# One task graph for everything behind the second run, and fold weights converted straight into SBUF

## The chip, the cores and the metric

The kernel runs on one core of a Trainium2 chip. The metric is the device time of one execution in microseconds. The kernel before takes 986.05 us, the median of three runs (982.78 to 986.43). The profile shown here is of one execution of 987.92 us; its span, from the first to the last instruction, is 986.2 us, so 1.7 us lie outside.

## What is computed

Three stages follow one another: a recurrent attention with a decaying state (4 batches, 8 heads, 768 steps, head size 48), and two gated blocks over the 3072 rows of 384 features that it gives.

```
state = zeros(B, H, D, D)
for t in range(S):                          # S = 768
    cur = einsum('bhd,bhe->bhde', u * k[t], v[t])
    y[t] = einsum('bhd,bhde->bhe', r[t], state + cur)
    state = w * state + einsum('bhd,bhe->bhde', k[t], v[t])
x = y as (3072, 384)
m = ((x @ w_a) * (x @ w_b)) @ w_out         # 384 -> 1536 -> 384
h = ((m @ w1) * (m @ w2)) @ w3              # 384 -> 1024 -> 1024
return h @ w_out2                           # 1024 -> 384
```

The MoE weights arrive as 64-bit floats. The kernel turns them into 32-bit ones with integer operations and then splits every matmul operand into a high part in fp32r and a low part (the rest), so that a product takes three matmuls: high by high, high by low, low by high.

## The kernel before

The sequence is cut into six chunks of 128 steps. A **unit** is one batch of one chunk (24 units; chunk 0 is done apart, so 20 go through the general path). A unit's attention is a chain: the scores on TensorE (L485), mask and diagonal on VectorE (L496, L502), the product with the state and with v on TensorE (L521, L525), evacuation as high and low part into `xt` (ScalarE L561 and L562, VectorE L563 and L564), the state update (TensorE L586, ScalarE L593, VectorE L603). GpSimd prepares r, k and the diagonal for the next unit (L457 to L478). When four units are done, six small DMAs (L570, `y_shuffle`) bring the odd rows of `xt` in place.

The **first block** works chunk by chunk (q = 0 to 5). For each of 12 feature tiles f, `ab_mm` makes two banks of 9 matmuls each (L736), ScalarE and VectorE multiply and split them (L755, L761, L762, L767), and `m_mm` adds 9 matmuls into the three banks `m` (L789 to L791). A finished chunk goes to DRAM (`m_d`).

The **second block** doesn't use w1 and w2 as they are: sums of slices of them (`T_OPS`, five groups g, `sums`) are multiplied with sums of slices of m (`S_OPS`), which saves matmuls; and w3 and the last weights are multiplied with each other once, in eight **folds** of 24 matmuls (L1079), so that one product (L1262 to L1264, called o here) remains. It runs over three pairs of chunks (L1159).

Weights are converted by `Stream`: SyncE loads a `raw` tile of 512 KB, VectorE makes the 32-bit value in three operations (L112, L126, L129), ScalarE rounds the high part and makes two checks (L142, L148, L163), VectorE makes the low part (L162). In the second half of the stream (`add_second`) there are 34 such conversions: 12 of w1 and w2, 6 of the last weights (`wo2`) and 16 of w3 (`w3T`). All results go to DRAM: w1 and w2 to `w12_d`, from where `sums` loads them again, the others with their two parts to `wo2_d` and `w3_d`, from where they come back for the folds.

What sets the order: up to chunk q = 4 of the first block everything is written out by hand. A list of runs (0 with its first six tiles; 1; 0 with the other six; 2; 3; 4) gives the main sequence, `merge` puts the slots of the next chunk's attention between its slots in equal steps, and the steps of conversions and sums likewise (`late`). From q = 5 on, everything (the last chunk, the folds, the second block) is a list of `Task`s with engine, duration, dependencies, buffers and a priority. The function `plan` orders them greedily: again and again it gives an engine the ready task that can start first, ties by priority. A task's end may be later than the engine's time for it by `extra`, which stands for a DMA's flight. Between the two parts the pools `att` and `stg` are released, and a pool `mid` takes their place.

Each engine runs its own instructions strictly in the order in which they were written.

## Time and profile before

| | us |
|---|---|
| median of three runs | 986.05 |
| profiled execution | 987.92 |
| its span | 986.2 |
| TensorE busy / VectorE busy / ScalarE busy / GpSimd busy | 895.8 / 569.4 / 370.7 / 240.7 |
| mean granted clock of TensorE | 0.947 |

The engines' busy times are sums over the span and hide that it has stretches with different limits. In the table of stretches each engine has its busy time and in brackets its number of instructions; PEclk is the granted clock of TensorE, where 1.00 is its upper level of 2.4 GHz. A matmul record is longer than the time that a matmul takes in a row of them, since matmuls are pipelined; what one takes is read from the chain, where a row of n of them stands with its whole duration.

### The profile page before, as it was taken

What the parts mean: (1) busy time and instruction counts of PE and PEld (TensorE: products, weight loads), DVE (VectorE), ACT (ScalarE), POOL (GpSimd) and SP (SyncE); (2) the same over time, 40 slices, a digit from 0 to 9 for tenths busy, and PEclk for the clock granted to TensorE, in tenths of its full rate; (3) what the DMA queues carried; (4) which work ended last, traced back from release to release, by engine and by line L of the source; (5) the groups of instructions that cost most, each with busy time, mean ns of one, the idle gap of its engine ahead of it and who ended that gap; (6) DMA issues with size and microseconds to landing.
All of it is one profiled execution on the core that took longest, in us unless ns stands there. A gap on an engine that the chain in (4) does not pass through costs nothing.

```text
span 986.2 us, 13053 instructions
## 1 busy us (share of the span) xinstructions
PE 895.8 (91%) x4827; PEld 747.3 (76%) x4827; DVE 569.4 (58%) x901; ACT 370.7 (38%) x830; POOL 240.7 (24%) x242
## 2 busy tenths in 40 slices
PE   8777999978796888999999967999999999999996
PEld 7566788867664666888888856888878788888996
DVE  8998964467676884545444403223569757845442
ACT  3554654235344544333232212223335233333232
POOL 2213200044020220645144001111534523212010
PEclk9888999989878788999999988999999999999998
DMA  8454531167578677325442381422655634324001
GB/s 264 162 174 137 154 107 43 47 212 190 174 249 241 210 218 204 141 82 182 128 142 81 104 308 68 158 96 96 230 156 164 197 116 131 107 91 155 6 33 67
DMA packets 55846, 143.60 MB, mean 146 GB/s; under 512 B 5536, under 2 KB 22688, under 8 KB 55776
## 3 DMA queue, kind: packets, MB, share of 16 engines
q1 hardware_dynamic: 55776, 142.70, 45.3%
q8 instruction: 40, 0.66, 0.3%
q14 instruction: 30, 0.25, 0.1%
HBM read 106.11 MB, written 34.60 MB: 143 GB/s over the span
## 4 chain that ended last, share of the span: by engine, by line
PE 60%; DVE 14%; DMA 14%; ACT 5%; issue 4%; POOL 1%; SPq 1%; DVEq 0%; ACTq 0%; POOLq 0%
PE ab L736 21%; PE ab L1159 9%; PE m L789 3%; PE m L791 3%; PE m L790 3%; PE at L1159 3%; PE at L1079 3%; DMA raw<-in_w3T_dram 3%; PE o L1262 3%; PE o L1263 3%; PE o L1264 3%; DVE cvt L126 2%; DMA raw<-in_wo_dram 2%; DMA r<-m_d 2%; DMA raw<-in_w_dram 1%
## 5 line engine op out<-in xcount | busy, mean ns | idle before, releaser
L762 ACT CAST gh<-ab 128x512 fp32r<-128x512 f32 x60 | 35.2, 587 | 167.9 <-DVE ab L761 151.8
L789 PE MATMUL m<-gh,woh 128*128 128x512 f32 x216 | 87.9, 407 | 2.5 <-DVE g L797 2.0
L1232 DVE TENSOR_TENSOR qx<-qx,ab 128x512 f32<-128x512 f32 x101 | 67.6, 685 | 39.1 <-PE ab L1159 31.8
L791 PE MATMUL m<-gh,wol 128*128 128x512 f32 x216 | 86.0, 398 | 0.8 <-DVE wol L162 0.8
L790 PE MATMUL m<-gl,woh 128*128 128x512 f32 x216 | 86.4, 400 | 0.0
L761 DVE TENSOR_TENSOR ab<-g,ab 128x512 f32<-128x512 f32 x60 | 41.7, 696 | 73.4 <-PE ab L736 72.5
L457 POOL TENSOR_TENSOR rk<-rk,tr 112x512 f32<-112x512 f32 x16 | 22.0, 1377 | 251.6 <-DMA rk<-in_rkT_dram 156.0
L1170 POOL TENSOR_TENSOR qx<-qx,qx 128x512 f32<-128x512 f32 x30 | 41.9, 1405 | 145.6 <-DVE qx L1232 135.2
L1254 DVE TENSOR_TENSOR gl<-qx,gh 128x512 fp32r<-128x512 f32 x48 | 37.5, 782 | 46.3 <-ACT gh L1252 46.2
L736 PE MATMUL ab<-xt,wab0h 128*128 128x512 f32 x144 | 50.5, 434 | 13.0 <-DVE gl L767 10.7
L755 ACT COPY g<-ab 128x512 f32<-128x512 f32 x60 | 34.9, 582 | 71.7 <-PE ab L736 71.7
L1252 ACT CAST gh<-qx 128x512 fp32r<-128x512 f32 x48 | 29.8, 621 | 80.1 <-PE o L1263 78.3
L736 PE MATMUL ab<-xt,wab1h 128*128 128x512 f32 x144 | 49.7, 429 | 9.5 <-ACT g L1034 9.5
L1226 ACT ACTIVATE qx<-ab 128x512 f32<-128x512 f32 x60 | 35.6, 599 | 57.1 <-PE ab L1159 26.7
L767 DVE TENSOR_TENSOR gl<-ab,gh 128x512 fp32r<-128x512 f32 x60 | 41.3, 689 | 26.7 <-ACT gh L762 26.6
L112 DVE TENSOR_SCALAR cvt<-raw 128x512 int32<-128x512 int32 x61 | 29.4, 481 | 45.5 <-DMA raw<-in_w3T_dram 18.2
L789 PEld LDWEIGHTS m<-gh,woh 128*128 128x128 f32 x216 | 41.7, 193 | 13.2 <-DVE g L797 2.5
L791 PEld LDWEIGHTS m<-gh,wol 128*128 128x128 f32 x216 | 41.8, 193 | 10.3 <-DVE wol L162 1.2
L1141 POOL TENSOR_TENSOR qx<-r 128x512 f32<-128x512 f32 x18 | 26.4, 1479 | 92.3 <-DMA m_d<-qx 33.4
L126 DVE SCALAR_TENSOR_TENSOR cvt<-raw,cvt 128x512 int32<-128x512 int32 x61 | 47.8, 784 | 1.2
L790 PEld LDWEIGHTS m<-gl,woh 128*128 128x128 f32 x216 | 41.7, 193 | 8.3
L736 PE MATMUL ab<-xt,wab3h 128*128 128x512 f32 x144 | 46.5, 404 | 0.0
(274 smaller groups left out, 2330.7 us busy)
## 6 DMA issues: line engine op xcount, KB each, us to landing
tg<-t_d SPq DMA_DIRECT2D x45, 640.0 KB, 3.9
natt<-in_nat_dram SPq DMA_DIRECT2D x20, 576.0 KB, 6.1
rk<-in_rkT_dram SPq DMA_DIRECT2D x24, 448.0 KB, 5.1
raw<-in_wab_dram SPq DMA_DIRECT2D x18, 512.0 KB, 3.9
raw<-in_w3T_dram SPq DMA_DIRECT2D x16, 512.0 KB, 4.9
w_d<-s SPq DMA_DIRECT2D x16, 512.0 KB, 3.6
w<-w_d SPq DMA_DIRECT2D x16, 512.0 KB, 4.4
t_d<-s SPq DMA_DIRECT2D x15, 512.0 KB, 2.6
```

The lines of the kernel that those rows point to most:

```text
L126: nc.vector.scalar_tensor_tensor(out=f, in0=w[:, :, 1], scalar=-0x40000000, in1=f, op0=ALU.bitwise_and, op1=ALU.bitwise_or)
L736: mm(ps, lhsT=w[i][:, k, cs], rhs=x[:, j, k, :], start=(n == 0), stop=(n == 3 * KD - 1))
L761: nc.vector.tensor_tensor(out=t["b"], in0=g, in1=t["b"], op=ALU.mult)
L767: nc.vector.tensor_tensor(out=gl, in0=t["b"], in1=gh, op=ALU.subtract)
L789: mm(m_ps[q][k], lhsT=wh[:, j, cs], rhs=gh, start=first, stop=False)
L790: mm(m_ps[q][k], lhsT=wh[:, j, cs], rhs=gl, start=False, stop=False)
L791: mm(m_ps[q][k], lhsT=wl[:, j, cs], rhs=gh, start=False, stop=last)
L1159: mm(bank, lhsT=x, rhs=y, start=(start and n == 0), stop=(stop and n == 2), skip_group_check=True)
L1170: mu = use(task(eng, D_TT if inner else D_P, lambda e=e, dst=dst, xa=xa, xb=xb: e.tensor_tensor(out=dst(), in0=xa(), in1=xb(), op=ALU.mult ...
L1226: e = use(task("ACT", D_A, lambda bv=bv, b=bank[c], s=s: nc.scalar.activation(out=bv.ap, in_=b.ap, func=ACTF.Copy, scale=float(s)), [pt], ...
L1232: e = use(task("DVE", D_TT, lambda bv=bv, b=bank[c], s=s: nc.vector.tensor_tensor(out=bv.ap, in0=bv.ap, in1=b.ap, op=ALU.add if s > 0 else ...
L1254: lo = use(task("DVE", D_TT, lambda x=x, bh=bh: nc.vector.tensor_tensor(out=bh.ap[1], in0=x(), in1=bh.ap[0], op=ALU.subtract), [hi], p0), ...
```

## The change

From the third run on (0 with its other six tiles) everything goes into the same list of tasks: the attention units of chunks 2 to 5 (priority -1000 and upwards, ahead of everything), the chunks 0, 2, 3, 4 and 5 of the first block (`block1`), the 12 conversions of w1 and w2 and the sums made of them (priority 9000, behind everything), and then what was planned already. The first two runs stay as they were.

- `plan` knows a DMA's size: transfers queue behind one another at 5 us per MB and land 2 us later; `extra` is gone.
- The sums of weight slices go from GpSimd (L827) to VectorE, slice by slice (128x128): 72 additions, and 80 splits into two parts with a store of 128 KB each, where there were 22 splits of up to four slices.
- The last weights and w3 are converted into the SBUF tiles that the folds read. `wo2_d` and `w3_d` are gone, and with them 11.5 MB written and 11.5 MB read. Their conversions have priorities around those of chunk q = 5.
- `att` is released by a task (`freed`) that waits for all units and all sums; `stg` stays. The second block's inputs are in other, smaller tiles.
- The o products have priorities inside the second block's groups instead of behind all of them; the last of the eight is cut by batches, so that the first batch can be evacuated earlier.
- The count of the checks becomes a task of the second block.

```diff
-        t.end = at + t.dur + t.extra
+        t.end = at + t.dur
+        if t.size:
+            dma = max(dma, t.end) + t.size * DMA_MB
+            t.end = dma + DMA_0
...
-        runs = [(0, range(SPLIT), 1), (1, range(NF1), None), (0, range(SPLIT, NF1), 2)]
-        runs += [(q, range(NF1), q + 1) for q in range(2, NB - 1)]
+        runs = [(0, range(SPLIT), 1), (1, range(NF1), None)]
...
+        for u in range(U0, NU):
+            c, b = divmod(u, B)
+            pu = -1000.0 + 10 * u
...
+            sc = use(task("PE", 1.35, lambda u=u, bt=bt: picked(bt, lambda: scores(u)), ready_r.get(u, []) + after, pu, bt),
+                     rk_b[u])
...
+                ev = use(task("DVE", 0.84, lambda u=u, h=h: a_diag(u, h), [ev] + ready_d.get(u, []), pu), ba, dg_b[u])
+            by = Buf(at_s, none)
+            y = use(task("PE", 2.3, lambda u=u, by=by: picked([by], lambda: y_mm(u)), [ev] + s_up.get(u - B, []), pu + 1,
+                         [by]), rk_b[u], nat_b[u], ba)
...
+                x_in[c].append(use(task("SP", 0.4, lambda c=c: y_shuffle(c), list(x_in[c]), pu + 3, size=0.13),
+                                   x_b[c], y3_b[c]))
...
+        for n, (q, fs) in enumerate([(0, range(SPLIT, NF1))] + [(q, range(NF1)) for q in range(2, NB)]):
+            mb = Buf(m_s, none)
+            t_ab, t_m = block1(q, fs, 200.0 * n, x_b[q], x_in.get(q, []), mb, [m_last])
...
+            ld = task("SP", 0.1, load, loads[-1:], prio, [br], size=0.52)
+            loads.append(ld)
+            x = use(task("DVE", 0.52, b1, [ld], prio, [bc]), br)
+            x = use(task("DVE", 0.80, b2, [x], prio), br, bc)
+            x = use(task("DVE", 0.80, b3, [x], prio), br, bc)
+            s = use(task("ACT", 0.85, square, [ld], prio, [bq]), br)
+            s = use(task("ACT", 0.90, sign, [s], prio), bq)
...
+            h = use(task("ACT", D_A, hi, [x] + list(after), prio, into if not after else []), bc, *into)
+            return use(task("DVE", 0.8, lo, [h], prio), bc, *into)
...
-            ops = list(ops_on(get, nc.gpsimd, L_OPS if left else T_OPS))
...
+                t = use(task("DVE", 0.25, add, [x[1], y[1]], prio, [b] if new else []), x[2], y[2], b)
...
+        freed = task("none", 0.0, hand_over, units + sum_tasks, 0)
...
+            wo2_l.append(convert(N_SUM + j, flat(wo2)[:, j * 512:(j + 1) * 512], None, R5 - 60 + 2 * j,
+                                 lambda i=i, z=z: [t[:, z * 512:(z + 1) * 512] for t in wo2_get(i)], after=[freed]))
...
+                ld.append(convert(N_SUM + 6 + 2 * i + j, flat(w3T[i])[:, s], None, R5 - 40 + 12 * i + j,
+                                  lambda b3=b3, s=s: [flat(t)[:, s] for t in b3.ap], [b3], after=ld))
...
-                    ot = use(task("PE", 12 * 0.177, go, [lo, fold_end[f]] + ([ot] if z else []), base + 5000 + 10 * n + z,
-                                  [bo] if z == 0 else []), bh, bo)
+                    p0, deps = base + (240 + 40 * z if n == 0 else 950 + 36 * z), [lo, fold_end[f]]
```

How the instructions move is read at three places. The first is VectorE in chunk q = 2 of the first block, while chunk 3's attention runs. Before, conversions of w3 stand there with their low parts (L162), each triple closed up between the product and the split of one feature tile (L761, L767):

```order
L162 TENSOR_TENSOR s<-cvt,s 128x512
L112 TENSOR_SCALAR cvt<-raw 128x512
L126 SCALAR_TENSOR_TENSOR cvt<-raw,cvt 128x512
L129 SCALAR_TENSOR_TENSOR cvt<-raw,cvt 128x512
L761 TENSOR_TENSOR ab<-g,ab 128x512
L162 TENSOR_TENSOR s<-cvt,s 128x512
L112 TENSOR_SCALAR cvt<-raw 128x512
L126 SCALAR_TENSOR_TENSOR cvt<-raw,cvt 128x512
L129 SCALAR_TENSOR_TENSOR cvt<-raw,cvt 128x512
L767 TENSOR_TENSOR gl<-ab,gh 128x512
```

In the changed kernel it is conversions of w1 and w2 (L1062, L1066, L1070), one operation at a time where the unit's chain (L504, L510, L582, L583, L622) leaves room:

```order
L914 TENSOR_TENSOR ab_2411<-g_2429,ab_2411 128x512
L1066 SCALAR_TENSOR_TENSOR cvt<-raw,cvt 128x512
L504 TENSOR_TENSOR a_sc<-at,mask 128x512 x2
L510 COPY_PREDICATED a_sc<-ident,dg 128x512 x2
L919 TENSOR_TENSOR gl_2459<-ab_2411,gh_2458 128x512
L914 TENSOR_TENSOR ab_2465<-g_2475,ab_2465 128x512
L1070 SCALAR_TENSOR_TENSOR cvt<-raw,cvt 128x512
L479 TENSOR_REDUCE dg<-pr 128x8
L919 TENSOR_TENSOR gl_2499<-ab_2465,gh_2498 128x512
L582 TENSOR_TENSOR y_2255<-at,y_2255 112x128
```

What moved: the sixteen w3 conversions left this place, and the attention's operations stand ahead of the rest of a triple.

The second place is ScalarE at the start of chunk q = 5. Before, the first high parts of the second block's inputs (L1150, which read `r`, the loaded m) stand between the chunk's first evacuation of a bank (L1034) and the next steps of its tiles (L1037, L1034):

```order
L1008 COPY qx_4823<-m_4222 128x512
L1034 COPY g_4840<-ab_4813 128x512
L1150 CAST qxa<-r 128x512 x3
L1037 CAST gh_4861<-ab_4829 128x512
L1034 COPY g_4875<-ab_4846 128x512
L1037 CAST gh_4890<-ab_4864 128x512
```

In the changed kernel the chunk's evacuations (L913, L916) and fold weights' high parts (L1083, which read a converted tile) share the place, and the first input of the second block (L1341) comes only behind three folds' evacuations (L1269):

```order
L916 CAST gh_4854<-ab_4797 128x512
L913 COPY g_4857<-ab_4808 128x512
L916 CAST gh_4871<-ab_4844 128x512
L913 COPY g_4883<-ab_4860 128x512
L1083 CAST w_4895<-cvt 128x512
L1269 CAST wf0h<-at_4821 128x384
L1083 CAST w_4895<-cvt 128x512
L913 COPY g_4945<-ab_4920 128x512
L916 CAST gh_4959<-ab_4885 128x512
```

What moved: the instructions that wait for the loaded m left the front of ScalarE's queue, and ones that wait for VectorE's conversions came in.

The third place is SyncE's queue at the same point. Before, it issues all fold weights (L1056, L1070) and the second block's first inputs (L1130) in a row:

```order
L890 DMA l_d<-s 128x256
L1056 DMA wo_4780<-wo_d 128x1536
L1056 DMA wo_4782<-wo_d 128x1536
L1056 DMA wo_4784<-wo_d 128x1536
L1056 DMA wo_4786<-wo_d 128x1536
L1070 DMA w_4788<-w_d_72 128x1024
L1070 DMA w_4789<-w_d_72 128x1024
L1070 DMA w_4792<-w_d_73 128x1024
L1070 DMA w_4793<-w_d_73 128x1024
L1115 DMA tl<-l_d 128x1280
L1130 DMA r<-m_d_58 128x3x256 x2
L1130 DMA r<-m_d_59 128x3x256 x2
```

In the changed kernel the last `y_shuffle` (L589) is followed by five input tiles in pieces (L1319) and by raw weights (L1057):

```order
L589 DMA xt<-y_4055 16x2x512 x6
L1319 DMA qs_4360<-m_d_58 128x256
L1319 DMA qs_4360<-m_d_59 128x256
L1319 DMA qs_4360<-m_d_58 128x256
L1319 DMA qs_4360<-m_d_59 128x256
L1319 DMA qs_4368<-m_d_58 128x256
L1319 DMA qs_4368<-m_d_59 128x256
L1319 DMA qs_4368<-m_d_58 128x256
L1319 DMA qs_4368<-m_d_59 128x256
L1319 DMA qcvt_4384<-m_d_58 128x256
L1319 DMA qcvt_4384<-m_d_59 128x256
L1057 DMA raw<-in_wo_dram 128x512 x2
```

What moved: 1.3 MB of pieces and two raw tiles stand where 7.5 MB of whole tiles stood.

## Rows read from the trace of the kernel before

**Rows 1.** The page: busy time, share of span, instructions.
```profile
PE 895.8 (91%) x4827; PEld 747.3 (76%) x4827; DVE 569.4 (58%) x901; ACT 370.7 (38%) x830; POOL 240.7 (24%) x242
```
**Rows 2.** Table of stretches: start:end, length, busy (instructions), PEclk, DMA, GB/s.
```profile
core 0: us, PE busy (x) PEld busy (x) DVE busy (x) ACT busy (x) POOL busy (x), PEclk, DMA share, GB/s
183.25:398.42 215.17, 175.79 (x978) 139.54 (x978) 146.68 (x240) 96.44 (x251) 49.45 (x45) 0.87 0.65 200
398.42:565.00 166.58, 166.58 (x978) 136.36 (x977) 76.26 (x126) 53.25 (x122) 65.02 (x95) 1.00 0.38 127
565.00:597.04 32.04, 18.12 (x71) 14.08 (x69) 5.69 (x15) 6.38 (x12) 1.15 (x1) 0.80 0.75 279
597.04:705.00 107.96, 107.96 (x508) 94.34 (x509) 32.65 (x48) 26.20 (x48) 21.28 (x15) 0.98 0.34 113
705.00:986.20 281.20, 267.02 (x1279) 231.44 (x1277) 168.73 (x237) 95.99 (x167) 72.81 (x51) 0.99 0.36 116
```
**Rows 3.** The same table for the first block's first matmuls (line 736).
```profile
183.25:398.42 215.17, 93.62 (x343) 69.32 (x343) 0.87 0.65 200
398.42:565.00 166.58, 99.50 (x411) 76.25 (x411) 1.00 0.38 127
```
**Rows 4.** The same table for instructions on the banks m; PE first.
```profile
183.25:398.42 215.17, 45.13 (x171) 33.40 (x171) 1.88 (x3) 1.56 (x3) 0.87 0.65 200
398.42:565.00 166.58, 49.49 (x199) 36.71 (x198) 0.00 (x0) 3.31 (x6) 1.00 0.38 127
```
**Rows 5.** Chain that ended last: start, us, what; rows of equal matmuls.
```profile
177.09 4.12 PE ab L736 x18
...
611.68 4.19 PE at L1079 x24
```
**Rows 6.** Waits from 183.25 to 398.42: who <- whom: us, times, longest.
```profile
POOL rk L457 <- DMA rk<-in_rkT_dram: 112.1, 6, 34.0
...
DVE cvt L112 <- DMA raw<-in_w3T_dram: 18.2, 12, 3.4
ACT s L142 <- DMA w_d<-s: 17.6, 7, 6.0
...
PE at L485 <- DVE s L603: 11.7, 4, 5.2
...
PE ab L736 <- DVE gl L767: 10.7, 2, 5.8
PE at L525 <- DVE a_sc L502: 9.6, 5, 4.5
```
**Rows 7.** Chain that ended last, from 568 to 597 us.
```profile
568.70 2.63 DMA l_d<-s
...
574.16 10.79 DMA w<-w_d
...
584.97 9.83 DMA r<-m_d
...
594.87 1.14 ACT qxa L1150 x2
```
**Rows 8.** Groups of instructions: busy us, mean ns, idle before and its releasers.
```profile
L112 DVE TENSOR_SCALAR cvt<-raw 128x512 int32<-128x512 int32 x61 | 29.4, 481 | 45.5 <-DMA raw<-in_w3T_dram 18.2 <-DMA raw<-in_w_dram 15.5 <-DMA raw<-in_wo_dram 6.7
L126 DVE SCALAR_TENSOR_TENSOR cvt<-raw,cvt 128x512 int32<-128x512 int32 x61 | 47.8, 784 | 1.2
L129 DVE SCALAR_TENSOR_TENSOR cvt<-raw,cvt 128x512 int32<-128x512 int32 x61 | 45.4, 745 | 1.2
L827 POOL TENSOR_TENSOR tw<-wa 128x128 f32<-128x128 f32 x32 | 15.0, 501 | 97.2 <-DMA wa<-w_d 94.3 <-DVE gl L767 2.9
```
**Rows 9.** Single lines: duration ns min/median/max, first and last start.
```profile
L889 DVE TENSOR_TENSOR s<-tw,s x22: 282/692/1402, 408.7 to 569.2; 128x512 fp32r<-128x512 f32 x16, 128x384 fp32r<-128x384 f32 x5, 128x128 fp32r<-128x128 f32 x1
L1152 DVE TENSOR_TENSOR qw4l<-qx,qw4h x5: 685/1181/1793, 668.3 to 834.1; 128x512 fp32r<-128x512 f32 x5
L570 SPq DMA_DIRECT2D xt<-y x30: 585/592/762, 98.2 to 558.1; - x30
```
**Rows 10.** Timeline at the end: start, us, engine, line, operation [idle before].
```profile
977.78 0.34 PE L1264 MATMUL o<-wf1h,gl 128*128 128x384 f32 x1
979.48 0.48 ACT L1277 COPY qx<-o 128x384 f32<-128x384 f32 x1 [2.42 <-DMA out_dram<-qx]
979.99 0.56 DVE L1275 COPY qx<-o 128x384 f32<-128x384 f32 x1 [2.27 <-ACT qx L1277]
```

More of the change, by code (lines that the diff above doesn't have):

```diff
@@ L278, in rwkv_moe_kernel @@
     l_d = dram.tile([128, 5, 2, 128], F32, name="l_d")
-    wo2_d = dram.tile([128, 2, NF2 * DM], F32, name="wo2_d")
-    w3_d = [dram.tile([128, 2, NF2 * 128], F32, name=f"w3_d{i}") for i in range(NF2)]
     def flat(ap):
@@ L898, in rwkv_moe_kernel, with task, use, run_tasks @@
-        second = []
+        tasks = []
+        def task(*a, **k):
+            t = Task(*a, **k)
+            for b in t.bufs:
+                b.users.append(t)
+            tasks.append(t)
+            return t
+        def use(t, *bufs):
+            for b in bufs:
+                b.users.append(t)
+            return t
+        def run_tasks():
+            plan(tasks)
+            for t in tasks:
+                t.end = 0.0
+            tasks.clear()
+        D_TT, D_A, D_P, MM = 0.70, 0.60, 1.45, 0.2275
@@ new lines, in rwkv_moe_kernel, with g_get, gg_get, ps_get @@
+        CONV = 9000.0
+        def g_get(key):
+            return gp.tile([128, TB], F32, tag=key, name=key)
+        def gg_get(key):
+            return tuple(gp.tile([128, TB], F32R, tag=f"g{p}{key}", name=f"g{p}{key}") for p in "hl")
+        def ps_get(key):
+            return psp.tile([128, 512], F32, tag=key, name=key)
+        def none(key):
+            return key
+        banks = [Slot(f"ab{k}") for k in range(3)]
+        at_s = [Slot(f"at{k}") for k in range(2)]
+        g_s = [Slot(f"g{k}") for k in range(2)]
@@ new lines, in rwkv_moe_kernel, with m_close, ev @@
+        gg_s = [Slot(k) for k in range(3)]
+        m_s = [Slot(("m0", "m1", "m2"))]
+        def m_close(q, m, mb, prio, pool, get):
+            out = []
+            for k in range(KD):
+                b = Buf(pool, get)
+                def ev(k=k, b=b):
+                    if q == 0:
+                        nc.vector.tensor_tensor(out=b.ap, in0=m_ps[q][k], in1=m_part[0][:, k, :], op=ALU.add)
+                    else:
+                        nc.scalar.copy(out=b.ap, in_=m_ps[q][k])
+                e = use(task("ACT" if q else "DVE", D_A if q else D_TT, ev, [m], prio, [b]), mb)
+                out.append(use(task("SP", 0.1, lambda k=k, b=b: nc.sync.dma_start(out=m_d[q][:, k, :], in_=b.ap), [e],
+                                    prio, size=0.256), b))
+            return out
@@ L916, in rwkv_moe_kernel @@
                 late += [lambda: None] * (len(late) // LATE)
-            if n == 2:
-                st.split(len(st.jobs))
-                k = len(st.jobs)
-                add_second()
-                second = [step] * (len(st.jobs) - k + 2)
-                for g in range(NG + 1):
-                    second += sums(g)
-            if n >= 2:
-                share = len(second) * len(main) // sum(
-                    3 * len(r[1]) for r in runs[n:]) if n < len(runs) - 1 else len(second)
-                late, second = second[:share], second[share:]
@@ new lines, in rwkv_moe_kernel, with put @@
+        first = len(st.jobs)
+        N_SUM = first + 4 * KD
+        for i in range(4):
+            for k in range(KD):
+                def put(f, i=i, k=k):
+                    for x in range(2):
+                        nc.sync.dma_start(
+                            out=w12_d[4 * i + x:4 * i + x + 3:2, :, k, :].rearrange("j p c -> p j c"),
+                            in_=f[:, x * 256:(x + 1) * 256].rearrange("p (j c) -> p j c", j=2))
+                done[i, k] = convert(first + i * KD + k, w12[i, :, k, :], put, CONV + 100 * i + k)
@@ L1047, in rwkv_moe_kernel @@
-        md_last = m_close(q, m_t[NF1 - 1], 10 * NF1)
-        f_dep = []
-        w_t, wo2_t, w3_t = {}, {}, {}
-        def wo2_load(p, i):
-            def go():
-                t = wo2_t[p, i] = mid.tile([128, 4, DM], F32R, tag=f"x{2 * p + i}", name=f"wo2{p}{i}")
-                nc.sync.dma_start(out=flat(t).bitcast(F32), in_=wo2_d[:, p, i * 4 * DM:(i + 1) * 4 * DM])
-            return task("SP", 0.1, go, [], -5, extra=5)
-        wo2_l = [wo2_load(p, i) for p in range(2) for i in range(2)]
@@ L1061, in rwkv_moe_kernel, with wo2_get @@
-        w3_s = [Slot(k) for k in range(2)]
+        R5 = 200.0 * (NB - 2)
+        ab_b, m_t, md_last = t_ab, t_m, d
+        o_slot = Slot(("m0", "m1", "m2", "at1"))
+        w_t, wo2_t = {}, {}
+        def wo2_get(i):
+            if i not in wo2_t:
+                wo2_t[i] = [mid_p[0].tile([128, 4, DM], F32R, tag=f"x{2 * i + p}", name="wo2") for p in range(2)]
+            return [flat(t) for t in wo2_t[i]]
+        wo2_l = []
+        for j in range(6):
+            i, z = divmod(j, 3)
+            wo2_l.append(convert(N_SUM + j, flat(wo2)[:, j * 512:(j + 1) * 512], None, R5 - 60 + 2 * j,
+                                 lambda i=i, z=z: [t[:, z * 512:(z + 1) * 512] for t in wo2_get(i)], after=[freed]))
```

489 lines of the change are left out of this document (302 added, 187 removed).

## The prediction

> **What bounds the kernel now.** I read the page's busy times first: TensorE is busy for 91% of the span, nothing else for more than 58% [rows 1]. So TensorE's own work is the floor, and the question is where it is not working, or working at its lower clock. The table by stretches answers that [rows 2]. I cut it where the program changes: up to 183.25 us the first two runs, which stay as they are; to 398.42 the stretch of chunks 0 and 2 of the first block in which all 34 late conversions run; to 565 the next chunks with sums; to 597 the change of pools; to 705 chunk 5 with the folds; then the second block. From 398 to 565 and from 597 to 705 TensorE is busy all the time at a clock of 1.00 and 0.98. From 183 to 398 it is busy for 176 of 215 us at 0.87, and from 565 to 597 for 18 of 32 us at 0.80. The second block loses little. The waits then say what the first bad stretch lacks [rows 6]: TensorE stands before scores, products and `ab` for VectorE, and VectorE stands before a conversion for its raw tile (L112) while ScalarE waits for the store of an earlier result. These waits of a few us each sit in queues that the attention's chain shares. In the second bad stretch the chain is one piece [rows 7]: a store of sums (2.6 us), then 10.8 us for the fold weights and 9.8 us for the loaded m, and then ScalarE's first split of that m, behind which the evacuations of chunk 5 are queued.
>
> **What TensorE needs.** A row of 18 matmuls of 512 columns takes 4.12 us, 0.229 us each; a row of 24 of 384 columns takes 4.19 us, 0.175 us each [rows 5]. The price of the attention comes from the stretch without idle time: 166.58 us less 411 + 199 = 610 matmuls [rows 3, 4] at 0.229 us (139.7 us) leaves 26.9 us for the other 978 - 610 = 368, or 0.073 us each [rows 2]. With that each stretch has a floor at the full clock:
>
> - 183 to 398: 343 + 171 = 514 matmuls give 117.7 us, 464 of attention 33.9 us: 151.6 us instead of 215.2, so 63.6 us too long.
> - 398 to 565: 166.6 us, nothing to gain.
> - 565 to 597: 69 of its 71 matmuls are of 512 columns: 15.8 us instead of 32.0, 16.2 us too long.
> - 597 to 705: 508, of which 8 x 24 = 192 are folds: 72.4 + 33.6 = 106.0 us instead of 108.0.
> - From 705: 1279, of which 3 x 2 x 8 x 12 = 576 are o: 161.0 + 100.8 = 261.8 us, then 8.1 us from the last matmul to the end [rows 10]; instead of 281.2, 11.3 us too long.
>
> With 183.25 us ahead, the floor is 183.25 + 151.6 + 166.6 + 15.8 + 106.0 + 261.8 + 8.1 = 893.2 us of span. No TensorE work is taken away; all that the change can do is to come nearer to that.
>
> **The change, part by part.** *One graph instead of merged lists.* In the stretch from 183 to 565 the units' operations come first and everything else fills in. Whether a plan holds on the chip can be read from the part that is planned already: from 597 on, 2.0 + 11.3 = 13.3 us are lost on 367.8 us of work, 3.6%. The task durations written in the code lie near the trace's for what I can compare (a conversion's first operation 0.52 against 0.48 us, the other two 0.80 against 0.78 and 0.75 [rows 8]). I take 3.6% of the 334.0 us from 183 to 597: **12 us** lost where 79.8 were. Bounds: 0 (the stretch from 398 on lost nothing, with the same units and tiles), and all of the 79.8.
>
> *What runs beside the attention.* VectorE was busy for 147 of 215 us there [rows 2]. Of the conversions only the 12 of w1 and w2 and the first of `wo2` remain, at 0.48 + 0.78 + 0.75 = 2.0 us each [rows 8], and no low parts but those of the sums. The 22 of w3 and `wo2` that are moved cost VectorE 2.0 + 0.69 = 2.7 us each [rows 8, 9], some 59 us, which go out of a stretch where VectorE is late and into chunk 5, where it is busy for 33 of 108 us.
>
> *Sums on VectorE.* GpSimd took 0.50 us for one addition [rows 8]. On VectorE no such row exists; a split of one slice took 0.28 us, one of four 0.69 [rows 9]. I take 0.28 for 72 additions and 80 splits: 43 us instead of 15, spread over the 330 us of chunks 0 to 4. That adds 9% to VectorE's load there and is hidden as long as VectorE's queue isn't late; nothing in the 398 to 565 stretch (76 of 167 us busy) speaks against it. ScalarE splits slices too and was busy for a third of its time.
>
> *SyncE.* The 58 further stores and the pieces of m make 379 DMAs in all where there were 339. One issue takes SyncE 0.59 us in `y_shuffle`, whose six take 3.6 us [rows 9]; the plan counts 0.4 us for them and 0.1 for others. So a chunk's `xt` lands some 3 us later than planned. Behind the shuffle on SyncE stand the next units' r, k and v. For chunks 3 to 5 the attention is done early (its priority is ahead of all), which hides it; for chunk 2, whose block follows at once, I count **2 us**, inside the 12.
>
> *The change of pools.* Chunk 5 no longer waits for 7.5 MB: five input pieces and the raw tiles are queued, and ScalarE has the splits of m far behind. The 10.8 + 9.8 us go. Next late there would be the conversions themselves: 18 remain behind `freed`, each a load, three operations, a split, with two raw tiles. In the 215 us from 183 on, 34 were done, 6.3 us each at most; 18 at 6.3 us are 113 us against 106 us of TensorE's work. VectorE's load is 18 x 2.7 + 4 x 0.7 for the first `wo2` tiles + 33 = 84 of 106 us. That is tight but it is spread by priorities over the chunk, so I add **3 us** (bounds 0 and 113 - 106 + one fold's 4.2, so 11).
>
> VectorE's operations on two SBUF tiles beside GpSimd stretch from 0.69 to 1.79 us in L1152 [rows 9]; with 15 GpSimd additions in chunk 5 that is up to 15 x 1.1 = 16 us more for VectorE, the upper bound again. The Trainium skill (SBUF — State Buffer, Who interferes with whom) says that a VectorE instruction with two SBUF inputs and a GpSimd instruction that reads SBUF block each other for the whole instruction; it speaks against moving the sums and conversions to VectorE beside GpSimd's work. By it the sum would have 84 + 16 = 100 of 106 us, still no bound of its own, some 8 instead of 3 us lost; the maxima in the rows agree with it, the medians show that most instructions escape.
>
> *The second block.* Its order is planned as before. The o products now have places inside the groups, which gives TensorE work where one pair of chunks follows another. Of the 11.3 us I take half, **6 us** lost. At the end, the fourth evacuation waited for a store's buffer (2.4 us [rows 10]); the cut by batches spreads the four, **2 us** won of the tail's 8.1 (bounds 0 and 3). The count's task costs under 1 us and TensorE one small matmul.
>
> Sum: 893.2 + 12 + 3 + 6 - 2 = 912.2 us of span. With 1.7 us outside, 913.9; the profiled execution stands 1.9 us above the median, so **912 us** as a median, 7.5% less.
>
> **The rivals.** *Conversions cost what they cost* (faster, by less). If TensorE's 63.6 us are lost to conversions as such, by VectorE and ScalarE waiting in order for raw tiles, each of the 34 takes 1.9 us of TensorE wherever it stands, since 34 remain. Then it is 893.2 + 63.6 + 6 - 2 = 960.8, or 960 as a median. For it: the waits for raw tiles [rows 6]. Against: most of TensorE's own waits name the attention's chain, and in chunk 5 there is no such chain. Something between, near 935, is likelier than the whole.
>
> *All units are slow* (slower). The loss was 63.6 us in 8 units, 8 us each, while much else ran on VectorE. Now conversions or small sums run beside all 16, and each in-order wait of VectorE holds up mask, diagonal and evacuation, and with them the next scores. At 8 us for each unit the time is 893.2 + 127 + 6 - 2 = 1024. It is slower than before from (986.2 - 897.2) / 16 = 5.6 us a unit on. Against it: eight units beside the sums of before lost nothing.
>
> *The gap stays.* `freed` waits for all units and all sums, and if the sums, last in priority, end late, `wo2` and the folds begin late and nothing covers the end of the chunk. The gap's 16 us come back: 928. For it: SyncE's longer queue of stores [rows 9]. Against: TensorE has chunk 5's tiles to do meanwhile, which don't need the pool.
>
> **How the numbers follow.** The forecast has 64%, its own range 895 (hardly any loss) to 930 (with the third rival's gap, given 10% of its own and counted here as its upper end). Between 930 and 962, by conversions, 18%. Above but still faster or unchanged 4%. Slower 4%, by units. The range goes from 895 to 955, which leaves out some 5% below and 13% above. A measurement can tell some 0.5% here; faster by more than that is 64 + 10 + 18 = 92%, of which I move 2 to slower for what I may not see in so large a rewrite: 0.90, within it 0.04, slower 0.06.
>
> **What would show it.** Right: from 183 us on TensorE's clock at 1.00 in every slice with busy shares of 9 and more, the second block beginning near 640 us instead of 705, no waits of ScalarE for loaded m at chunk 5's start. Conversions as such: waits of VectorE for raw tiles and a clock below 1 inside chunk 5. Units: waits of TensorE's scores and products for VectorE in chunks 3 to 5. I am wrong if the clock in the new stretch stays under 0.95, or if the folds end after chunk 5's last tile.

## The result and the profile after

The changed kernel takes 908.3 us (904.7 to 908.8, four runs) where the kernel before, on the same chip, takes 985.7 (982.8 to 986.4): a ratio of 0.921, 95% interval 0.918 to 0.924. Repeated later beside the last experiment it took 904.6 us (902.5 to 907.0), ratio 0.917 (0.915 to 0.920). The forecast was 912. The profiled execution shown here is one of 908.81 us, 907.0 of them its span.

The page first, busy times and then TensorE's granted clock in 40 slices:

```profile
PE 869.5 (96%) x4827; PEld 731.2 (81%) x4827; DVE 601.3 (66%) x1031; ACT 372.8 (41%) x865; POOL 204.0 (22%) x170
...
PEclk9698899999999999999999999999999999999998
```

TensorE has the same 4827 matmuls as in [rows 1] and is busy for 96% of a shorter span. VectorE has more to do than before (601 instead of 569 us) and GpSimd less. From the sixth slice on, at 113 us, the clock's digit is 9 up to the last. The table of stretches answers [rows 2]; it is cut where the runs written by hand end (184.70), where chunk 5 begins (510.28) and where the second block begins (618.20, just behind the start of its first matmul at 617.79):

```profile
core 0: us, PE busy (x) PEld busy (x) DVE busy (x) ACT busy (x) POOL busy (x), PEclk, DMA share, GB/s
184.70:510.28 325.58, 323.40 (x1985) 265.11 (x1986) 233.25 (x457) 133.76 (x361) 89.12 (x72) 1.00 0.51 156
510.28:618.20 107.92, 107.92 (x518) 94.57 (x518) 60.56 (x92) 49.80 (x105) 13.10 (x9) 1.00 0.25 86
618.20:907.00 288.80, 274.65 (x1306) 237.82 (x1305) 170.21 (x245) 96.20 (x170) 71.84 (x52) 0.98 0.38 121
```

In the first of them TensorE stands still for 2.2 of 325.6 us at the full clock, in the second not at all. VectorE is busy for 233 of 326 us, 72%, where it was 68% in the bad stretch of [rows 2]; TensorE hardly waits for it all the same. The waits of the first stretch (who, for whom: us, times, longest) are all that is left of TensorE's waits in [rows 6]:

```profile
PE m L809 <- DVE gl L919: 1.5, 1, 1.5
PE ab L755 <- ACT g L913: 0.6, 1, 0.6
```

The chain of [rows 7] is gone: chunk 5's tiles run while the fold weights are converted. What remains is the second block. From 618.20 to the end of its last matmul (898.7 us) are 280.5 us, with 730 matmuls at 0.229 and 576 at 0.175 us [rows 5], 268.0 us of work: 12.5 us more than these prices give. TensorE's waits there are 5.7 us, nearly all at the changes from one pair of chunks to the next; the longest two lines:

```profile
PE o L1455 <- DVE gl L1445: 3.7, 2, 3.1
PE ab L1350 <- DVE qx L1423: 1.6, 3, 0.9
```

Not all of the 12.5 us can be won: the last experiment runs the same matmuls without a wait, and they take some 4 us more than the prices of [rows 5]. The tail, from the last matmul to the end, is 8.3 us.

### The profile page after: what moved, and what is told of

It reads as the page before. It is cut to its first block, busy times and chain, and to the rows that moved or that the text cites. A ratio compares the mean times of both kernels' runs of the same rounds, so it can differ in the third digit from the quotient of the medians.

```text
span 907.0 us, 13215 instructions
## 1 busy us (share of the span) xinstructions
PE 869.5 (96%) x4827; PEld 731.2 (81%) x4827; DVE 601.3 (66%) x1031; ACT 372.8 (41%) x865; POOL 204.0 (22%) x170
## 4 chain that ended last, share of the span: by engine, by line
PE 83%; DVE 10%; DMA 2%; issue 2%; ACT 1%; SPq 0%; DVEq 0%; ACTq 0%
PE ab L755 31%; PE ab L1350 12%; PE m L808 5%; PE m L810 5%; PE m L809 5%; PE at L1350 4%; PE at L1258 4%; PE o L1453 3%; PE o L1455 3%; PE o L1454 3%; PE at L533 3%; PE at L493 2%; PE at L529 2%; DMA rk<-in_rkT_dram 1%; DVE qx L1423 1%
## 5 line engine op out<-in xcount | busy, mean ns | idle before, releaser
L914 DVE TENSOR_TENSOR ab<-g,ab 128x512 f32<-128x512 f32 x54 | 37.5, 695 | 71.1 <-PE ab L755 63.2
L916 ACT CAST gh<-ab 128x512 fp32r<-128x512 f32 x54 | 31.7, 586 | 100.5 <-DVE ab L914 100.5
L1445 DVE TENSOR_TENSOR gl<-qx,gh 128x512 fp32r<-128x512 f32 x48 | 40.3, 844 | 45.8 <-ACT gh L1443 45.7
L1361 POOL TENSOR_TENSOR qx<-qx,qx 128x512 f32<-128x512 f32 x27 | 36.6, 1357 | 141.1 <-DVE qx L1423 108.4
L913 ACT COPY g<-ab 128x512 f32<-128x512 f32 x54 | 31.8, 588 | 83.6 <-PE ab L755 83.6
L1417 ACT ACTIVATE qx<-ab 128x512 f32<-128x512 f32 x55 | 32.6, 600 | 74.3 <-PE ab L1350 73.1
L486 POOL TENSOR_TENSOR kn<-natt,tnat 128x384 f32<-128x384 f32 x13 | 13.9, 1071 | 152.6 <-PE at L605 152.6
L919 DVE TENSOR_TENSOR gl<-ab,gh 128x512 fp32r<-128x512 f32 x54 | 37.1, 687 | 14.9 <-ACT gh L916 14.6
L755 PE MATMUL ab<-xt,wab2h 128*128 128x512 f32 x144 | 45.5, 397 | 0.0
L755 PE MATMUL ab<-xt,wab5h 128*128 128x512 f32 x144 | 45.1, 394 | 0.0
L755 PE MATMUL ab<-xt,wab4h 128*128 128x512 f32 x144 | 45.1, 394 | 0.0
```

Source lines behind the costliest of these rows:

```text
L755: mm(ps, lhsT=w[i][:, k, cs], rhs=x[:, j, k, :], start=(n == 0), stop=(n == 3 * KD - 1))
L914: mu = use(task("DVE", D_TT, lambda x=bg, y=bb: nc.vector.tensor_tensor(out=y.ap, in0=x.ap, in1=y.ap, op=ALU.mult), [ea, b], p0 + 2), bg, bb)
L919: nc.vector.tensor_tensor(out=x.ap[1], in0=y.ap, in1=x.ap[0], op=ALU.subtract)
L1361: mu = use(task(eng, D_TT if inner else D_P, lambda e=e, dst=dst, xa=xa, xb=xb: e.tensor_tensor(out=dst(), in0=xa(), in1=xb(), op=ALU.mult ...
L1417: e = use(task("ACT", D_A, lambda bv=bv, b=bank[c], s=s: nc.scalar.activation(out=bv.ap, in_=b.ap, func=ACTF.Copy, scale=float(s)), [pt], ...
L1445: lo = use(task("DVE", D_TT, lambda x=x, bh=bh: nc.vector.tensor_tensor(out=bh.ap[1], in0=x(), in1=bh.ap[0], op=ALU.subtract), [hi], p0), ...
```

## The experiments

Four questions were open: whether conversions beside the attention cost TensorE anything, whether the gap of [rows 7] was the loads', whether the plan's new DMA model matters, and where the second block's 12.5 us go. What converting the fold weights straight into SBUF is worth by itself was not run.

**More conversions beside the attention.** The changed kernel with 22 conversions repeated in the stretch of chunks 0 to 4:

```diff
...
+        for j in range(6):
+            again(j, N_SUM + j, flat(wo2)[:, j * 512:(j + 1) * 512])
+        for j in range(16):
+            again(6 + j, N_SUM + 6 + j, flat(w3T[j // 2])[:, j % 2 * 512:(j % 2 + 1) * 512])
...
         sum_tasks = [t for t in tasks if t.prio >= CONV]
```

> The changed kernel with 22 further conversions (the six of the last weights and the sixteen of w3 a second time, each with its high and low part and a store to a DRAM buffer that nobody reads), at the lowest priority beside the attention. Theory (the graph's order is what freed TensorE: whatever runs beside the units now fills gaps of VectorE): 908 to 915 us, although VectorE has 22 x 2.7 = 59 us more, 292 of the 326 us from 185 to 510. Rival (each conversion takes 1.9 us of TensorE wherever it stands, as 63.6 us were lost to 34 of them): 908 + 22 x 1.9 = 950 us.

Measured: 944.1 us (943.5 to 946.4), ratio 0.952 (0.947 to 0.957). By the number the rival has it; by the place it has not. The table of stretches of this kernel:

```profile
175.00:350.00 175.00, 174.31 (x1175) 143.33 (x1175) 140.81 (x247) 78.56 (x210) 62.00 (x50) 1.00 0.61 189
350.00:525.00 175.00, 173.97 (x927) 142.36 (x922) 123.03 (x262) 83.34 (x215) 21.26 (x17) 1.00 0.59 189
...
575.00:600.00 25.00, 19.67 (x93) 16.92 (x92) 19.33 (x33) 18.67 (x41) 0.00 (x0) 0.90 0.67 220
600.00:625.00 25.00, 19.20 (x65) 18.56 (x65) 13.46 (x23) 11.13 (x27) 0.00 (x0) 0.64 0.36 124
625.00:650.00 25.00, 16.32 (x72) 15.36 (x71) 15.68 (x29) 11.89 (x28) 6.03 (x4) 0.85 0.27 92
```

While the 22 further conversions ran (their high parts stand from 299.8 to 510.9 us), TensorE lost 1.7 of 350 us. The loss comes behind them, from 575 to 650, and there TensorE waits for fold weights alone:

```profile
PE at L1275 <- ACT w L1084: 19.8, 8, 3.6
```

The rest of the loss is mostly the clock between these waits (0.64 to 0.90): the 190 fold matmuls and 37 others from 575 to 650 are 42 us of work at the prices of [rows 5] and took 55. (L1275 and L1084 are L1258 and L1083 of the changed kernel.) So I formed another theory: a conversion costs TensorE nothing where it runs, but `freed` waits for the last of them, and the fold weights' conversions begin late. The third rival of the prediction described that mechanism. It can be told from a price by halving the dose.

**Half as many.** The same with 11 further conversions:

```diff
-        for j in range(16):
+        for j in range(5):
             again(6 + j, N_SUM + 6 + j, flat(w3T[j // 2])[:, j % 2 * 512:(j % 2 + 1) * 512])
```

> The changed kernel (908.3 us) with 11 further conversions beside the attention (6 of the last weights, 5 of w3) whose results go to DRAM and are not used; with 22 of them it took 944.1. Theory, cover: conversions fill VectorE's spare time and cost TensorE nothing there; they only put off the release of the pool. The sums ended at 414.7 us in the changed kernel and at 531.8 with 22 further ones, 5.3 us for each, so with 11 they end near 473, some 16 us behind the last unit (457), and the folds end near 617, just when chunk 5's last tile does (618): 908 to 915. Rival, price: each conversion costs TensorE (944.1 - 908.3) / 22 = 1.6 us: 926.

Measured: 905.4 us (903.6 to 907.9), not distinguishable from the changed kernel. Half the dose cost nothing and the whole one 36 us, so there is no price for each. When the fold weights' high parts are made (count: shortest, median and longest in ns, first and last start in us) shows why; first the changed kernel, then 11, then 22 further conversions:

```profile
L1083 ACT CAST w<-cvt x16: 605/622/624, 482.4 to 581.3; 128x512 fp32r<-128x512 f32 x16
L1083 ACT CAST wo<-cvt x6: 606/620/623, 460.1 to 476.2; 128x512 fp32r<-128x512 f32 x6
```
```profile
L1084 ACT CAST w<-cvt x16: 604/622/625, 513.4 to 591.4; 128x512 fp32r<-128x512 f32 x16
...
L1084 ACT CAST wo<-cvt x6: 619/622/626, 487.6 to 506.8; 128x512 fp32r<-128x512 f32 x6
```
```profile
L1084 ACT CAST w<-cvt x16: 617/618/623, 570.1 to 646.7; 128x512 fp32r<-128x512 f32 x16
L1084 ACT CAST wo<-cvt x6: 622/622/624, 540.1 to 564.6; 128x512 fp32r<-128x512 f32 x6
```

The 22 conversions behind `freed` take 104 to 121 us, about 5 us each. Begun at 460 or at 488 us they end before chunk 5's last matmul of `ab` (611 us in the changed kernel); begun at 540 they end at 647, 36 us behind that, and the time is 36 us longer. Chunk 5 covers a delay of 27 us without a loss.

**The same conversions in the merged order.** In the kernel before, those of w3 and the last weights moved behind the sums:

```diff
...
                 for g in range(NG + 1):
                     second += sums(g)
+                second += [lambda: (add_rest(), step())] + [step] * 24
...
+                share = 14 if n == 2 else share
```

(`add_rest` holds the 22 conversions; the last line leaves the first stretch to the other 12; eight empty steps stand between these and the sums.)

> The kernel before, merged by hand as it is, with the 22 conversions of w3 and the last weights moved behind the sums, so that only the 12 of w1 and w2 stand in the stretch from 183 to 398 us. If the hand-written merge makes each conversion cost TensorE time wherever it stands, the loss moves to the later chunks and the time stays at 986 within 8 us. If the loss was VectorE being overfull in that one stretch (147 of 215 us busy), two thirds of it go: 63.6 x 22/34 = 41 us, some 945 us.

Measured: 987.3 us (985.4 to 990.9), ratio 0.998 (0.995 to 1.001). Its stretches:

```profile
200.00:275.00 75.00, 61.86 (x392) 49.57 (x393) 49.87 (x83) 31.44 (x83) 24.48 (x20) 0.95 0.61 181
275.00:450.00 175.00, 175.00 (x1068) 143.82 (x1067) 85.28 (x140) 59.51 (x142) 74.66 (x107) 1.00 0.39 129
450.00:600.00 150.00, 100.77 (x450) 78.70 (x449) 82.49 (x143) 62.16 (x147) 14.43 (x11) 0.81 0.70 230
```

In the kernel before TensorE was busy for 149.9 of the 175 us from 275 to 450, and for 136.1 of the 150 from 450 to 600. Most of the loss has moved with the conversions, but the 49 us that TensorE stands still from 450 to 600 are of three kinds:

```profile
PE cnt_ps L1292 <- DVE ones L944: 14.8, 1, 14.8
PE ab L736 <- ACT g L1038: 11.9, 1, 11.9
PE at L525 <- DVE a_sc L502: 11.0, 3, 5.1
```

The first is the count of the checks, which stands ahead of chunk 4's last matmuls and waits until the last conversion is through; in the kernel before it waited 4.4 us. The second is the gap of [rows 7], 9.5 us there. The third and three smaller ones, 22.6 us in all, are the waits behind VectorE's and ScalarE's queues: 1.0 us for each of the 22 conversions. In the kernel before such waits were 39.2 us, 1.2 for each of the 34. From the start of the third run to chunk 5's first matmul the two kernels take 395.9 and 392.9 us; without the waits for the count it is 391.5 and 378.1, so 13 of the 63.6 us came back and 50 did not. So in the merged order conversions do cost, in both places where they were put, much as the first rival said; in the planned order they don't. I take that for the difference between a step of work put after a fixed number of slots and one operation put where its engine has room; no run separates this from the units' priority, which the plan brings too.

**The gap alone.** The kernel before with nothing but the plan's DMA model changed, so that transfers queue behind one another:

```diff
-        t.end = at + t.dur + t.extra
+        t.end = at + t.dur
+        if t.extra:
+            dma = max(dma, t.end) + t.extra * DMA_MB
+            t.end = dma + DMA_0
...
-                         extra=2.5)
+                         extra=0.262)
...
```

(`extra`, a flight in us before, is now a size in MB at every DMA of the plan, so that the flight also goes by the size.)

> The kernel before with one part of the change alone: its plan counts DMAs as queueing behind one another at 5 us per MB and 2 us to land, instead of a fixed flight each. Theory (the gap from 565 to 597 us came from ScalarE's splits of m being planned ahead of chunk 5's evacuations because the plan thought that m would be there): the splits move back, 10 to 16 of the 16.2 us come back, 970 to 976 us. Rival (the gap is the change of pools itself and the 7.5 MB that have to come): 986 us.

Measured: 973.2 us (972.2 to 973.9) beside 990.1 (985.3 to 995.6) of the kernel before on the same chip, ratio 0.981 (0.976 to 0.986). The stretch of [rows 7], first of the kernel before, then of this one:

```profile
575.00:600.00 25.00, 15.49 (x57) 12.21 (x56) 4.86 (x7) 5.66 (x10) 4.03 (x3) 0.77 0.83 312
```
```profile
575.00:600.00 25.00, 25.00 (x111) 20.64 (x110) 5.55 (x8) 6.46 (x11) 3.84 (x3) 0.99 0.76 284
```

The gap's stretch is full, with nearly the same bytes moved (7.1 instead of 7.8 MB). ScalarE now goes on to chunk 5's next step (L1043, L1037 of the kernel before) at 582.45 us, where it had stood until 595.92 behind the split of the loaded m, and that split (L1156) comes 31 us later:

```profile
582.45 0.59 ACT L1043 CAST gh<-ab 128x512 fp32r<-128x512 f32 x1 [2.31 <-DVE ab L1041]
613.17 1.66 ACT L1156 CAST qxa<-r 128x512 fp32r<-128x512 f32 x3
```

From chunk 5's first matmul to the second block's first it takes 108.0 us instead of 119.5, so 11.5 us of the 16.2 are this order's; of the rest the wait for the count (4.4 us) is still there. The whole span is 14.5 us shorter.

**The changed kernel without that model.** Each DMA lands on its own time, as if the queues were empty:

```diff
-            dma = max(dma, t.end) + t.size * DMA_MB
-            t.end = dma + DMA_0
+            t.end += t.size * DMA_MB + DMA_0
```

> The changed kernel with the queueing of DMAs taken out of its plan: each lands 2 us + 5 us per MB after its issue. Theory (little is queued at chunk 5 now, and raw loads are one by one): 906 to 914 us. Rival (without the queue in the plan the splits of m go to ScalarE's front again): 908 + 16 = 924 us.

Measured: 921.7 us (918.6 to 924.6), ratio 0.929 (0.923 to 0.934). The number is near the rival's, the place is another. First this kernel, then the changed one:

```profile
200.00:275.00 75.00, 69.64 (x508) 56.03 (x507) 64.51 (x102) 36.76 (x103) 37.32 (x30) 0.98 0.67 201
...
475.00:600.00 125.00, 125.00 (x585) 107.33 (x584) 79.65 (x123) 63.49 (x139) 16.64 (x11) 1.00 0.31 100
```
```profile
200.00:275.00 75.00, 74.30 (x562) 61.01 (x561) 66.42 (x108) 34.29 (x94) 36.90 (x31) 1.00 0.69 207
...
475.00:600.00 125.00, 123.55 (x584) 106.83 (x583) 75.45 (x112) 59.82 (x130) 16.65 (x11) 1.00 0.26 88
```

At chunk 5, where the gap was, nothing is lost. It is lost beside the attention, 5.4 instead of 0.7 us from 200 to 275, and in smaller pieces behind. There the plan puts operations before transfers that have not landed, the raw tiles of w1 and w2 above all: from 200 to 275 ScalarE waits for them for 24.7 us, in the changed kernel for 5.5. First this kernel, then the changed one:

```profile
ACT sq L1075 <- DMA raw<-in_w_dram: 24.7, 10, 5.5
```
```profile
ACT sq L1076 <- DMA raw<-in_w_dram: 5.5, 2, 4.9
```

TensorE's own waits in that stretch name VectorE; how each of them goes back to a raw tile, and what the smaller losses behind are due to, stays open.

**The sums on GpSimd.** Their 72 additions on the engine that did them before:

```diff
-                    nc.vector.tensor_tensor(out=b.ap, in0=x[0](), in1=y[0](),
+                    nc.gpsimd.tensor_tensor(out=b.ap, in0=x[0](), in1=y[0](),
...
-                t = use(task("DVE", 0.25, add,
+                t = use(task("POOL", 0.50, add,
```

> The changed kernel with the 72 additions of the sums on GpSimd, as in the kernel before (0.50 us each there), instead of VectorE. Theory: nothing waits for these additions, TensorE is busy in the whole stretch either way: 905 to 912. Rival: GpSimd's additions stretch VectorE's instructions on two SBUF tiles (0.69 to 1.79 us) in the stretch where VectorE is busy for 22 to 23 of 25 us; with 72 x 1.1 us at most, 79 us of VectorE in 215, the units and with them the scores come late: 920 to 940.

Measured: 904.8 us (901.5 to 907.6), no difference that can be told from the changed kernel (904.6 and 908.3). VectorE has 18 us less to do (582.8 instead of 601.3) and GpSimd 35 more, and TensorE is busy at the full clock in both. The engine for the sums doesn't matter here.

**The o products behind all groups.** The priorities of before the change, and nothing else:

```diff
-                    p0, deps = base + (240 + 40 * z if n == 0 else 950 + 36 * z), [lo, fold_end[f]]
+                    p0, deps = base + 5000 + 10 * n + z, [lo, fold_end[f]]
```

> The changed kernel with the o products' priorities as before the change: behind all groups of a pair of chunks. Theory of the prediction: the places inside the groups give TensorE work where one pair follows another and save about half of the 11.3 us that the second block lost, so without them 913 to 916. Rival: the second block's 13.6 lost us are VectorE's at the changes of pairs (24.0 of 25 us busy from 675 to 700 and from 775 to 800), and the o products only bring their splits (L1445) there too: 903 to 909.

Measured: 903.5 us (900.6 to 907.7), ratio 0.916 (0.912 to 0.920). The first theory, which is the prediction's, fails: without the places inside the groups the kernel is not slower. From the start of chunk 5's last matmul of `ab` with a high part of the weights to the last matmul of all, the changed kernel takes 287.5 us (611.2 to 898.7; repeated 287.0), this one 284.2. The medians of the whole time can't be told apart.

**No GpSimd in the second block.** Additions of m's slices and the products of columns go to VectorE:

```diff
...
-                    nc.gpsimd.tensor_tensor(out=bc.ap, in0=x[0](), in1=y[0](), ...
+                    nc.vector.tensor_tensor(out=bc.ap, in0=x[0](), in1=y[0](), ...
...
-                eng = "DVE" if inner else "POOL"
+                eng = "DVE"
...
```

> The changed kernel with the second block's additions (L1332) and products (L1361) on VectorE instead of GpSimd, which then does nothing there. Theory: at the changes of pairs VectorE is full because its splits last 1.2 to 1.8 us beside GpSimd's instructions instead of 0.69; about 14 of them between 675 and 702 us lose 1.1 us, some 13 us in two changes, while 10 additions and products more for VectorE are 7 us a change. The second block loses 6 to 10 instead of 13.6 us: 901 to 905. Rival: VectorE's own work is what counts and it grows by 50 x 0.69 = 35 us: 911 to 918.

Measured: 902.9 us (899.8 to 904.9), ratio 0.913 (0.910 to 0.917); the stretch named above takes 284.4 us. What it removes can be seen in the changed kernel's timeline at a change of pairs (start, us, engine, and what it does), first GpSimd's rows, then VectorE's, then TensorE's:

```profile
691.66 1.74 POOL L1332 TENSOR_TENSOR qs<-qs,qs 128x512 f32<-128x512 f32 x1
693.36 1.75 POOL L1332 TENSOR_TENSOR qs<-qs 128x512 f32<-128x512 f32 x1
695.19 1.60 POOL L1332 TENSOR_TENSOR qs<-qs,qs 128x512 f32<-128x512 f32 x1
```
```profile
692.17 1.78 DVE L1343 TENSOR_TENSOR qxb<-qcvt,qxb 128x512 fp32r<-128x512 f32 x1
693.88 1.78 DVE L1343 TENSOR_TENSOR qw5l<-qs,qw5h 128x512 fp32r<-128x512 f32 x1
695.58 3.42 DVE L1445 TENSOR_TENSOR gl<-qx,gh 128x512 fp32r<-128x512 f32 x2
698.93 0.68 DVE L1343 TENSOR_TENSOR qw5l<-qs,qw5h 128x512 fp32r<-128x512 f32 x1
```
```profile
695.57 0.34 PE L1454 MATMUL o<-wf1l,gh 128*128 128x384 f32 x1
699.06 0.44 PE L1455 MATMUL o<-wf1h,gl 128*128 128x384 f32 x1 [3.15 <-DVE gl L1445]
```

GpSimd and VectorE take turns: each of these VectorE instructions on two SBUF tiles lasts 1.7 to 1.8 us, and the next one without GpSimd, at 698.93, lasts 0.68. An o product stands in TensorE's queue behind such a split (L1445) and waits 3.15 us, and so do the products behind it. Then the clock is low; the stretch from 699 to 703 us of the same trace:

```profile
699.00:703.00 4.00, 3.94 (x13) 3.45 (x14) 3.93 (x8) 1.58 (x3) 0.48 (x1) 0.58 0.48 144
703.00:706.00 3.00, 2.11 (x9) 1.44 (x8) 3.00 (x4) 0.00 (x0) 0.80 (x1) 0.99 0.51 182
```

A granted clock of 0.58 is near the lower level of 1.2 GHz: 13 matmuls in 4 us, where 20 stand in the 4 us from 706 on. The group of these splits (count, busy us and mean ns) in the changed kernel and in this one:

```profile
L1445 DVE TENSOR_TENSOR gl<-qx,gh 128x512 fp32r<-128x512 f32 x48 | 40.3, 844 | 45.8 <-ACT gh L1443 45.7
```
```profile
L1445 DVE TENSOR_TENSOR gl<-qx,gh 128x512 fp32r<-128x512 f32 x48 | 32.8, 689 | 28.9 <-ACT gh L1443 28.7
```

The Trainium skill (SBUF — State Buffer, Who interferes with whom) says that a VectorE instruction with two SBUF inputs and a GpSimd instruction that reads SBUF block each other for the whole instruction; the rows of the two engines above agree. The gain, 3 us of the stretch, was less than the theory's 4 to 8. VectorE also got more work: in the whole kernel 66 instructions moved to it and its busy time is 622.4 us, where it was 601.3. At 0.69 us each they would have added 46; the difference is what its other instructions got shorter, as the splits above.

**Both, and the changed kernel once more.** The two edits together, on the same chip as the unaltered kernel:

> The changed kernel once more, unaltered, beside the next one on the same chip, since those with edits in the second block differ from it by less than 1%. Both theories: 904 to 909, as before (904.7 to 908.8); executions at a granted clock of 0.985 near 904.7, those at 0.977 near 908.4.

> The changed kernel with the second block's additions and products on VectorE and the o products behind all groups of a pair, the two edits that ran alone before (902.9 and 903.5, against 908.3 in another job). Theory: both losses are VectorE's at the changes of pairs. From the last tile of chunk 5 on, the changed kernel took 296 us, the one with o behind 292, the one without GpSimd 294; if the two gains add, 290 to 291: 5 us under the changed kernel of the same job, 899 to 904. Rival: the two edits remove the same collision, so 292 again: 3 to 4 us under it.

Measured: 904.6 us (902.5 to 907.0) unaltered and 896.2 (894.0 to 900.3) with both edits, ratios to the kernel before 0.917 (0.915 to 0.920) and 0.909 (0.906 to 0.911). This is 8.4 us less than the changed kernel, the fastest of all, and more than both theories gave. The same stretch takes 278.3 us where it took 287.0: a gain of 8.7, while each edit alone gained 2.6 to 3.3 in one execution, which the medians of the whole time don't show. The larger change of pairs, unaltered and then with both edits:

```profile
675.00:725.00 50.00, 45.38 (x218) 39.95 (x217) 37.45 (x48) 20.17 (x35) 21.26 (x14) 0.97 0.35 115
```
```profile
675.00:725.00 50.00, 49.92 (x237) 42.91 (x236) 37.46 (x61) 16.88 (x30) 0.00 (x0) 1.00 0.51 156
```

VectorE is as busy there as without the edits, and no wait of TensorE is left. Why the gains don't add up is told by the whole second block, from its first matmul to its last, in four kernels: unaltered, o behind, no GpSimd, both.

```profile
613.15:893.64 280.49, 274.47 (x1308) 237.97 (x1306) 169.59 (x245) 95.90 (x170) 71.81 (x52) 0.99 0.39 122
```
```profile
613.35:890.97 277.62, 272.12 (x1308) 236.74 (x1306) 168.82 (x245) 97.80 (x170) 72.26 (x52) 1.00 0.40 123
```
```profile
614.09:891.86 277.77, 273.57 (x1308) 237.33 (x1306) 187.79 (x297) 96.80 (x170) 0.00 (x0) 1.00 0.40 123
```
```profile
612.42:884.07 271.65, 271.57 (x1308) 237.03 (x1306) 185.68 (x297) 97.89 (x170) 0.00 (x0) 1.00 0.40 126
```

TensorE stands still for 6.0, 5.5, 4.2 and 0.1 us, and the same matmuls keep it busy for 274.5, 272.1, 273.6 and 271.6 us. With o behind, the waits are hardly shorter in sum, but the longest is 2.1 us (for a product of columns, L1361) instead of 3.15, and the stretch at half the clock is gone. With everything on VectorE, o still waits 1.2 us and a group 1.5 us for it. Only both together leave no wait. Only the tail is longer, 10.8 instead of 8.1 us.

## Why the prediction was right, and where its terms were off

The forecast, 912 with a range from 895 to 955, is 4 us above the first measurement and 7 above the repetition. Its mechanism is confirmed by the signs that it named, two excepted: the second block begins at 618 us, not near 640, and ScalarE waits once for a load of m. That the sum comes so near is luck for the greater part: the term for the graph was too large and the one for the second block too small.

- *The first two runs*, 183.25 us. Measured 184.7, with the same code.
- *One graph*, 12 us lost of 334. Measured about 1: from 184.70 to 510.28 stand 1153 matmuls of 512 columns at 0.229 and 832 of the attention at 0.073 us, 324.8 us of work in 325.6. The share of 3.6% was taken from the planned part of the kernel before, but what that part loses is the second block's own, and some of it is no loss but the price of its matmuls, as the last run shows. The lower bound, 0, was the right end.
- *Conversions beside the attention.* That they cost TensorE nothing where they stand is shown by 11 and by 22 further ones, which go to DRAM as w3 did before; so it is the order that freed this stretch, not the way round DRAM. The rival of 960 us is largely true of the merged order only. VectorE's waits for raw tiles fell from 40.4 us (18.2 [rows 6], 15.5 and 6.7 [rows 8]) to 1.1.
- *Sums on VectorE*, hidden: shown by moving them back to GpSimd.
- *SyncE*, 2 us inside the 12: less than 1 lost from 200 to 275.
- *The change of pools*, 3 us lost in chunk 5. Measured none: 192 folds and 326 matmuls of 512 columns are 108.3 us of work in 107.9. The last fold ends at 601 us, 10 before chunk 5's last matmul of `ab`. The estimate of 6.3 us for each conversion, "tight", was too high; 5 was measured. Against the sign that was named, ScalarE still waits once for a load of m (2.3 us, at the first of the last weights' high parts, at 460 us), which costs TensorE nothing.
- *The gap stays.* Not in this kernel, but 22 conversions more bring it back, at 36 us instead of 16: its condition, `freed` late by more than the cover, was described rightly.
- *The second block*, 6 us lost. Measured 12.5, and this step failed: "gives TensorE work where one pair of chunks follows another" was argued from TensorE's side alone. The splits of o need VectorE at just the time at which it is full, and a product in TensorE's queue that waits for its split holds up the rest. TensorE's waits in the block were 5.9 us before and are 5.7 now; put behind all groups, o costs some 3 us less. The 11.3 us that were to be halved were also too many: some 4 us of them are the price of the matmuls, 271.6 us where [rows 5] give 268. It begins at 618 us rather than the 638 of the sum; 6 us of that are work, 27 matmuls, that now stands behind the boundary.
- *GpSimd beside VectorE.* I priced it where the change put new work, in chunk 5, at up to 16 us; there it cost TensorE nothing. That "most instructions escape" was read too kindly: the L1152 row in [rows 9] has a median of 1.18 us, so at least half of its five were stretched. It costs in the second block, at the changes of pairs, where I had not looked because the change leaves those instructions as they are.
- *The tail*, 2 us won. Measured 8.3 instead of 8.1 us [rows 10], nothing won.
- *The fold weights straight into SBUF.* No run has the changed kernel without this part, so what it adds is not shown; further conversions to DRAM cost nothing beside the attention, and the model of the DMAs alone took 11.5 us of the gap's 16.2 away.

In sum: 11.2 us too much for the graph and 3.4 for the pools, 6.5 too little for the second block, 2.2 for the tail and 1.4 for the first two runs; together 4.5 of the 5.2 us between the 912.2 of the forecast span and the 907.0 measured.

## What to carry to other kernels

Before charging background work by the piece, ask what makes it cost: in the merged order here it was charged at both places, in the one planned by engine it was free until its end delayed the next thing that waited for all of it; so look for that wait and measure how much lateness the work beside it can cover. Where a product is moved forward to fill a gap, cost every step that feeds it on the engine that is late in that gap. Where VectorE is full for a short time, first look at what GpSimd does there: taking work from GpSimd onto VectorE can make TensorE's waits for VectorE shorter, as it did here together with the later o.

## What the runs showed that I had not expected

- GpSimd and VectorE, both on two SBUF tiles of 128x512, run in turn, 1.6 to 1.8 us each where VectorE alone takes 0.69. Where they meet like this, an addition on GpSimd takes more time from VectorE (1.1 us) than it would cost there (0.69).
- Two edits worth some 3 us each gave 8.7 together; in the block's rows these are 5.9 us of waits and 2.9 us for which the same matmuls were busy longer.
- A wait of TensorE of 3.15 us, in a stretch that was full at 1.00 before, was followed by 4 us at a granted clock of 0.58.
- Executions of one kernel differ by 4 us in the part before the change: from 0 to 184.7 us the granted clock was 0.91 in the first profile of the changed kernel and 0.94 in the repeated one, and the matmul of `ab` named above began at 611.2 and at 606.6 us. Edits in the second block are therefore compared from that matmul on.
